# Loads of w, a, b for chunks 4 and 5 issued by ScalarE, and the first weight product placed behind chunk 0's state update

## The chip, the cores and the metric

The kernel runs on one core of a Trainium2 chip. A core has five instruction queues: PE (TensorE, matrix products), DVE (VectorE), ACT (ScalarE), POOL (GpSimd) and SP (SyncE, which here only issues transfers). Each queue works in order: an instruction that has to wait holds up everything behind it on that queue. Queues meet through semaphores. The metric is the device time of the kernel in microseconds (us), lower is better.

## The reference

Two blocks follow each other. The first is a recurrence with a 40 x 40 state per batch and head, over 768 steps, for 4 batches and 8 heads:

```
for t in range(S):
    y[:, :, t] = einsum('bhd,bhde->bhe', r_t, state)
    Sa = einsum('bhde,bhe->bhd', state, a_t)
    state = state * w_t[:, :, None, :] - outer(Sa, b_t) + outer(v_t, k_t)
```

The second takes y as 3072 tokens of 320 features and computes `h = x @ w_in`, `g = h * cos(h)`, `out = g @ w_out`, with 2048 hidden features. The six inputs of the recurrence are float32. The two weight matrices arrive as float64, so the kernel itself has to turn each pair of 32-bit words into a float32.

## The kernel before

**Tiling.** Time is cut into 24 chunks of 32 steps (`C = 32`, `NCH = 24`). A chunk's inputs lie in SBUF as 128 partitions (4 batches x 32 steps) by 8 heads x 40. Within a chunk the recurrence becomes matrix products, for which a 32 x 32 triangular system per batch and head must be inverted. That is done for four chunks at a time by 31 pairs of small DVE operations (`inv_step`, L464 to L472), which end in a transpose into the tile `rt` (L476).

**Stages of a chunk.** `p1_w`, `p1_a`, `p1_b`, `p1_n` prepare the decay, a, b and the triangular system, for two chunks at once. `p2_in` copies v and r to padded tiles on POOL (`vp`, `rp`, L490), `p2_kn` scales k and copies v on POOL (`kn`, `vvm`, L497 and L498), `p2_v`, `p2_k`, `p2_g` turn them and form the products inside the chunk (`gram`; ACT copies `vT`, `rT`, `kT`, L514 to L521; DVE `ag` L541; ACT and DVE `vvm`, L546 and L547). The chain from chunk to chunk is `ch_t` (turn the state `qz`: PE `sT`, ACT `s`, L562), `ch_q` (`qps`), `ch_x` (`x0ps`, copied by ACT L599 and DVE L600), `ch_s` (`sps`, with `rt`; copied to `sm` by ACT L617 and DVE L622), and `ch_z` (`dps`; DVE adds to the state, `qz` L656, POOL scales it, `qz` L657, and the outputs go to `yt`, L663 and L668).

**The second block** is cut into pieces (`first_a`, `first_b`, `second`), which an explicit list of segments puts between the stages of the recurrence. They are the bulk of PE's work: the groups `ph` and `po`.

**Weights.** Each of the two matrices is converted in pieces of 128 x 512 (`rounded`, L220). One piece takes a fetch of its words by SP (`fetch`, L233), `taken` (DVE L241 and L242, ACT L245 and L247), `mantissa` (DVE L251, ACT L254) and `product` (DVE L257, then POOL L260, which sets the sign). These steps form one list, `w_steps`, and `step(work, of_inv, of_w)` (L342) takes `of_w` of them after each segment. For chunks 0 and 1 that number is 4, the second entry of `fill = (1, 4)` (L924). So after `ch_s` of chunk 0 come taken 0, taken 1, mantissa 0 and product 0, and after its `ch_z` the next four.

**Order of the loads.** `later(n, work)` (L339) issues a piece of work after n further segments. `load(c, names, via)` (L146) issues four transfers of 40 KB for each named input of chunk c, by SP unless `via` says otherwise. k, v and r of all chunks share one tile each; `landed` (L501) asks for those of the next chunk once both readers on POOL are through. Two lines matter here:

```
elif c >= 2 and c + 3 < NCH:                       # L800
    for m in range(6):
        later(8 + m // 3 if c == 2 else ..., lambda m=m: load(c + 2 + m % 2, "wab"[m // 2]))
...
step(seg, *fill, small=seg in (q, x, g, s, z, pn, pn4))   # L982
```

With c == 2 the first loads w, a, b of chunks 4 and 5: w4, w5 and a4 after the eighth further segment, a5, b4 and b5 after the ninth. The decay w of these chunks comes from a table `wd` in DRAM, which SP stores shortly before (L180). Between the two groups SP fetches the words of the first three weight pieces, and k, v, r of chunk 2 stand behind all of it.

**Completion semaphores.** The program as built gives the transfers of SP and ACT eight completion semaphores in turn, and each transfer waits until the one that used its semaphore before has landed. So at most eight transfers of the two queues are under way, and either queue can wait for the other's.

`N_PAD` (L897) and `busy` (L856) put idle matmuls into PE's stream at the start: 111 tiny ones (`pad`) in front of the first `sps`, and some of 512 columns.

Of the kernel before, what the change touches and what calls it, by code (L numbers as in the profile page):

```python
# [20 lines left out]
def kernel(  # L21
# [43 lines left out]
    nc = tc.nc  # L65
# [54 lines left out]
    for n, fill in (("w", 1.0), ("a", 0.0), ("b", 0.0)):  # L120
        for i in range(4):
            x = slice((i - 2) * H * DP, (i - 1) * H * DP)
# [23 lines left out]
    def load(c, names, via=nc.sync):  # L146
        for n in names:
            for i in range(B):
                at_c = src[n][i, :, c * C : (c + 1) * C, :]
                if n == "w" and c >= 4:  # L150
                    at_c = wd[c // 4][i, :, c % 4]
                via.dma_start(nat[n, c][blk[i], :, :D], at_c.rearrange("h t d -> t h d"))  # L152
# [186 lines left out]
    def later(steps, work):  # L339
        waiting.append([steps, work])  # L340

    def step(work, of_inv=0, of_w=0, small=False):  # L342


        before = list(waiting)
        work()
        G["small"] = small
        for w in before:
            w[0] -= 1
            if w[0] == 0:  # L350
                waiting.remove(w)
                w[1]()
        for steps, n in ((inv_steps, of_inv), (w_steps, of_w)):
            for _ in range(min(n, len(steps))):
                steps.pop(0)()


    def p1_w(c):
        ps = at("wT")
        for i in range(2):  # L360
            turned(ps[:, i], nat["w", c + i])
        if c < 4:

            for i in range(2):
                nc.scalar.copy(G["w1"][:, i, :, 0:1], b4(ps[:, i])[:, :, 0:1])
            nc.vector.memset(ps[:, :, ::C], 0.0)
        for i in range(2):
            wb = ring.tile([P, 4 * P + 1], F32, tag="wb", name="wb")
            if c < 4:
                nc.vector.tensor_tensor_scan(  # L370
                    wb[:, 1:], ps[:, i], flat(G["w1"][:, i]), 0.0, ALU.mult, ALU.add
                )
            else:
                nc.scalar.copy(wb[:, 1:], ps[:, i])
            wc = ring.tile([P, 4 * B], F32, tag="wc", name="wc")
            nc.gpsimd.tensor_copy(wc, wb[:, C::C])
            G["wb", c + i], G["wx", c + i], G["wc", c + i] = wb, b4(wb[:, : 4 * P]), wc
            if c >= 4:
                from_one(c + i)
        if c == 8:  # L380
            later(2, lambda: over_w(c, unpad(nat["w", c])))
        elif c >= 4:
            over_w(c, unpad(nat["w", c]))
# [18 lines left out]
    def p1_a(c):  # L402
        if c >= 4:
            ps = at("aps")
            for i in range(2):
                turned(ps[:, i], nat["a", c + i])
            for i in range(2):
                a_W(c + i, ps[:, i])
            over_w(c + 1, unpad(nat["w", c + 1]))
            return  # L410
        for c in range(c, c + 2):
            wn = ps_h.tile([P, 512], F32, tag="h", name="wn")
            aps = ps_o.tile([P, 512], F32, tag="o", name="aps")
            for j in range(4):
                nc.tensor.transpose(
                    wn[:, j * P : (j + 1) * P], G["wb", c][:, j * P + 1 : (j + 1) * P + 1], ident
                )
            from_one(c)
            turned(aps, nat["a", c])
            over_w(c, unpad(wn.rearrange("p (h d) -> p h d", h=H)))  # L420
            a_W(c, aps)
# [364 lines left out]
    def p1(c):  # L786


        def first_w():
            p1_w(c)  # L790
            if c == 4:
                later(1, lambda: load(6, "w"))

        def both_a():
            p1_a(c)
            if c == 4:
                later(1, lambda: load(7, "w"))
                for i in range(2):
                    later(1, lambda i=i: load(6 + i, "ab"))
            elif c >= 2 and c + 3 < NCH:  # L800
                for m in range(6):
                    later(
                        8 + m // 3 if c == 2 else (9 if c == 6 else 2) + m, lambda m=m: load(c + 2 + m % 2, "wab"[m // 2])
                    )

        return [first_w, both_a, lambda: p1_b(c), lambda: p1_n(c)]
# [8 lines left out]
    def p2(c):  # L815
        def last():
            p2_g(c)
            if c + 1 < NCH:
                later(1, lambda: p2_in(c + 1))

        return [lambda: p2_v(c), lambda: p2_k(c), last]
# [9 lines left out]
    with tc.manual_schedule():  # L831
# [53 lines left out]
        v, k, g = p2(0)  # L885
# [34 lines left out]
        for c in range(NCH):  # L920
            t, q, x, s, z = main(c)
            v, k, g = p2(c + 1) if c + 1 < NCH else [lambda: None] * 3
            q0 = c - c % 4 + 4
            fill, pn, pn4 = (1, 4), None, None  # L924
            if c == 0:
                segs = [s, z]
            elif c == 1:
                segs = [t, v, q, k, x, g, s, z]
            elif c == 2:
                segs, fill = [t, v, q, k, M, x, M, g, M, s, M, z, M, M], (0, 2)  # L930
            elif c == 3:
                pw4, pa4, pb4, pn4 = p1(4)
                pw, pa, pb, pn = p1(6)
                segs = [
                    t, pw4, M, q, pa4, M, x, lambda: scanned(2), M, s, pw, M, pb4, pa, M, pn4, M, z, M,
                    pb, v, pn, k, M, g,
                ]
                fill = (2, 3)
            elif c == 4:
                pw, pa, *p8 = p1(8)  # L940
                segs = [t, v, M, q, M, k, x, M, M, M, M, pw, s, M, z, M, g, M, pa, lambda: scanned(3)]
                fill = (2, 0)
            elif c == 5:
                pw, pa = p1(10)[:2]
                pb, pn = p8
                segs = [t, M, pb, q, M, pn, k, M, x, M, s, pw, v, M, z, M, g, M, pa, M]
            elif c % 4 == 0 and q0 < NCH:
                pb, pn = p1(q0)[2:]
                segs = [t, v, M, q, M, k, x, M, g, M, s, pb, M, z, M, pn, M, M]
                if q0 + 4 < NCH:  # L950
                    segs.insert(-1, lambda: scanned(c // 4 + 2))
            elif c % 4 == 1 and q0 < NCH:
                pw, pa = p1(q0 + 2)[:2]
                segs = [t, M, pw, q, M, x, k, M, s, v, M, z, M, pa, M, g, M, M]
            elif c % 4 == 2 and q0 < NCH:
                pb, pn = p1(q0 + 2)[2:]
                segs = [t, M, pb, q, M, pn, v, M, x, M, s, k, M, g, M, z, M, M]
            elif c % 4 == 3 and q0 + 4 < NCH:
                pw, pa = p1(q0 + 4)[:2]
                segs = [t, M, pw, q, M, x, k, M, s, v, M, z, M, pa, M, g, M, M]  # L960
            else:
                segs = [t, v, M, q, M, x, k, M, g, M, s, M, M, z, M, M]
            n = len(segs)

            goal = 8 * (c + 1) - (18 if c < 19 else 20)
            empty, places = 0, segs.count(M)
            if c > 3:
                empty = max(0, min(places - (goal - done), 2 if c < 8 else places))
                goal = max(goal, done + places - empty)
            place = 0  # L970
            if c == 19:
                shifted(N_PAD[c])
            for i, seg in enumerate(segs):
                while seg is s and ("rt", c) not in G:
                    if allowed(c):
                        piece(4, 0)
                    else:
                        inv_steps.pop(0)()
                while seg is pn4 and w_steps:
                    w_steps.pop(0)()  # L980
                if seg is not M:
                    step(seg, *fill, small=seg in (q, x, g, s, z, pn, pn4))  # L982
                    if c < 2 or c == 2 and not done:
                        busy({s: 6, q: 5, v: 4, k: 4, z: 4}.get(seg, 3))
                else:
                    place += 1
                    if place * empty // places > (place - 1) * empty // places:
                        continue
                    if allowed(c) and (c != 4 or done < 23):
                        piece(*fill)  # L990
                while i == n - 1 and c > 3 and done < goal and c != 4 and allowed(c):
                    piece(*fill)
                if seg is pn and (c == 3 or c > 4 and c % 4 == 2):
                    inv_steps.extend(inverse(q0))
# [36 lines left out]
```

## Time and profile before

| | us |
|---|---|
| median of 3 runs | 825.33 (822.83 to 826.02) |
| span of the profiled execution | 823.7 |
| PE busy | 746.9 (91%) |
| DVE busy | 509.3 (62%) |
| ACT busy | 383.8 (47%) |
| POOL busy | 201.3 (24%) |

The profile's own execution took 823.7 us from its first to its last instruction, 1.6 below the median of the runs. A busy share is an average over stages with different limits: what a change in one stage is worth has to be read from that stage. The chain of waits follows the work that ended last back through what released it. The timeline lists instructions by start, with their length and the idle time of their engine ahead of them. "SPq" and "ACTq" are the transfers issued by those queues; issuing is not counted as busy. Numbers such as L152 are lines of the kernel.

### The profile page before, as it was taken

Reading aid. Unit: us, or ns where it says so; the run is one execution under the profiler, and the core shown is the slowest. Engines: PE = TensorE matmul, PEld = TensorE weight load, DVE = VectorE, ACT = ScalarE, POOL = GpSimd, SP = SyncE. Lnnn points to the kernel's source line nnn. Section 1 sums busy time; section 2 is a strip of 40 time slices with the busy share of each in tenths; the row PEclk is TensorE's granted clock in tenths of the full one; section 3 lists DMA queues with packets and bytes.
Section 4 is the critical chain, followed back from the end, with each engine's and each line's share of the span. In section 5 each row is a group of like instructions: output and inputs, shape, how many; then the busy total and the mean of one; then the engine's idle time right before and its main releaser. Section 6 shows DMA issues by size and latency. Waiting matters only on the chain.

```text
span 823.7 us, 37673 instructions
## 1 busy us (share of the span) xinstructions
PE 746.9 (91%) x16832; PEld 571.3 (69%) x16832; DVE 509.3 (62%) x1081; ACT 383.8 (47%) x707; POOL 201.3 (24%) x352
## 2 busy tenths in 40 slices
PE   3656778899689999999999999999999999999997
PEld 2534456677467777778777777777787777777775
DVE  6987887859645599354797553895444874332231
ACT  1214676544244553545446446435635445363352
POOL 5315554430214023212221230330330222201000
PEclk9757799899789999999999999999999999999999
DMA  8456663244043322333223323214310212101000
GB/s 120 78 132 168 173 162 104 46 119 69 25 98 84 64 59 52 69 100 65 54 37 71 68 63 67 61 37 65 66 41 24 45 35 52 21 21 37 20 17 16
DMA packets 183297, 55.66 MB, mean 68 GB/s; under 512 B 157152, under 2 KB 178656, under 8 KB 183136
## 3 DMA queue, kind: packets, MB, share of 16 engines
q1 hardware_dynamic: 180560, 51.95, 29.2%
q8 instruction: 132, 2.16, 1.1%
q10 hardware_dynamic: 2320, 0.98, 0.6%
q0 software_dynamic: 256, 0.33, 0.2%
q14 instruction: 29, 0.24, 0.1%
HBM read 42.07 MB, written 11.14 MB: 65 GB/s over the span
## 4 chain that ended last, share of the span: by engine, by line
PE 63%; DVE 19%; ACT 6%; DMA 4%; issue 3%; SPq 3%; POOL 1%; DVEq 0%; ACTq 0%; POOLq 0%
PE ph L101 22%; PE po L101 20%; DVE inv_tmp L468 4%; DVE inv L472 4%; PE x0ps L101 3%; PE dps L101 3%; SPq L152 3%; PE gram L101 2%; DVE rw L391 2%; PE vT L326 2%; PE sps L101 2%; PE qps L101 1%; DVE turns L732 1%; PE nps L101 1%; PE sT L558 1%
## 5 line engine op out<-in xcount | busy, mean ns | idle before, releaser
L101 PE MATMUL po<-w_out_sb,gT 128*128 128x320 f32 x768 | 227.0, 445 | 0.0
L101 PE MATMUL ph<-xT,w_in_sb 128*128 128x256 f32 x768 | 189.5, 393 | 4.8 <-DVE gT L740 3.8
L101 PEld LDWEIGHTS po<-w_out_sb,gT 128*128 128x128 f32 x768 | 142.4, 193 | 55.9 <-issue 4.2
L101 PEld LDWEIGHTS ph<-xT,w_in_sb 128*128 128x128 f32 x768 | 142.3, 194 | 33.9 <-issue 13.9
L730 ACT ACTIVATE turns<-ph,rnd 128x512 f32<-128x512 f32 x96 | 63.8, 685 | 157.2 <-PE ph L101 156.7
L732 DVE SCALAR_TENSOR_TENSOR turns<-turns,ph 128x512 f32<-128x512 f32 x96 | 63.8, 684 | 109.2 <-ACT turns L730 108.9
L740 DVE TENSOR_TENSOR gT<-ph,turns 128x512 f32<-128x512 f32 x96 | 65.6, 685 | 36.3 <-ACT turns L737 36.3
L657 POOL TENSOR_TENSOR qz<-qz,wc 128x160 f32<-128x160 f32 x92 | 43.2, 489 | 163.1 <-DVE qz L656 162.6
L472 DVE TENSOR_TENSOR inv<-inv,inv_tmp 128x31 f32<-128x31 f32 (+15 forms) x186 | 72.0, 387 | 6.4
L468 DVE TENSOR_TENSOR inv_tmp<-u,inv 128x31 f32<-128x31 f32 (+15 forms) x186 | 70.0, 376 | 4.4
L736 ACT ACTIVATE turns<-turns 128x512 f32<-128x512 f32 x96 | 60.2, 627 | 23.3 <-DVE turns L732 23.3
L737 ACT ACTIVATE turns<-turns,half_pi 128x512 f32<-128x512 f32 x96 | 69.3, 722 | 3.1
L490 POOL COPY vp<-nat_v 128x320 f32<-128x320 f32 x25 | 12.5, 501 | 182.9 <-DMA nat_v<-in_v_dram 144.1
L101 PE MATMUL ph<-xT,w_in_tail 64*128 64x256 f32 x384 | 54.8, 404 | 0.0
L656 DVE TENSOR_TENSOR qz<-dps,qz 128x160 f32<-128x160 f32 x92 | 28.9, 315 | 33.9 <-PE dps L101 33.8
L391 DVE RECIPROCAL rw<-nat_w 128x320 f32<-128x320 f32 x20 | 42.8, 2142 | 0.1
L562 ACT COPY s<-sT 128x512 f32<-128x512 f32 x46 | 24.5, 584 | 37.6 <-PE sT L558 37.6
L101 PEld LDWEIGHTS ph<-xT,w_in_tail 64*128 64x128 f32 x384 | 33.3, 187 | 10.4 <-issue 6.6
L668 POOL TENSOR_TENSOR yt<-yt,wb 128x512 f32<-128x512 f32 x24 | 31.3, 1306 | 22.4 <-DVE yt L663 22.4
L546 ACT COPY vvm<-gram 128x256 f32<-128x256 f32 x24 | 8.8, 368 | 55.6 <-DVE ag L541 55.3
L101 PEld LDWEIGHTS sps<-x,rt 32*32 32x32 f32 x1536 | 18.1, 109 | 21.6 <-issue 16.5
L101 PE MATMUL sps<-x,rt 32*32 32x72 f32 x1536 | 23.0, 240 | 10.7 <-DVE rt L476 9.0
(118 smaller groups left out, 1070.1 us busy)
## 6 DMA issues: line engine op xcount, KB each, us to landing
words<-in_moe_w_in_dram SPq DMA_DIRECT2D x8, 512.0 KB
nat_k<-in_k_dram SPq DMA_DIRECT2D x96, 40.0 KB
nat_v<-in_v_dram SPq DMA_DIRECT2D x96, 40.0 KB
nat_r<-in_r_dram SPq DMA_DIRECT2D x96, 40.0 KB
xd<-yt SPq DMA_DIRECT2D x48, 80.0 KB
out_dram<-ot SPq DMA_DIRECT2D x24, 160.0 KB
nat_b<-in_b_dram SPq DMA_DIRECT2D x88, 40.0 KB
wd<-ws SPq DMA_DIRECT2D x5, 640.0 KB
```

The costliest lines, as they stand in the source:

```text
L101: nc.tensor.matmul(o, lhsT=lhsT, rhs=rhs, start=start, stop=stop, skip_group_check=True)
L391: nc.vector.reciprocal(rw, wn)
L468: nc.vector.tensor_tensor(tmp, u[:, j : j + 1, :j].to_broadcast([P, C - j, j]), x[:, j:, j : j + 1].to_broadcast([P, C - j, j]), ALU.mult,)
L472: nc.vector.tensor_tensor(x[:, j:, :j], x[:, j:, :j], tmp, ALU.subtract)
L656: nc.vector.tensor_tensor(z, pick(dp, 0, (2 * N72 + C, 2), (N72, 2), (1, D)), z, ALU.add)
L657: nc.gpsimd.tensor_tensor(z, z, wc.rearrange("p (f m b) -> p f m b", f=2, m=2)[:, :, :, bb] .unsqueeze(3).to_broadcast([P, 2, 2, D]), ALU. ...
L668: nc.gpsimd.tensor_tensor(yt.rearrange("p j b t -> p (j b) t"), yt.rearrange("p j b t -> p (j b) t"), wx, ALU.mult)
L730: nc.scalar.activation(n, u, ACTF.Identity, bias=rnd, scale=1.0)
L732: nc.vector.scalar_tensor_tensor(n, n, -ROUND, u, ALU.add, ALU.subtract)
L736: nc.scalar.activation(n, n, ACTF.Abs)
L737: nc.scalar.activation(n, n, ACTF.Sin, bias=half_pi, scale=-2.0 * math.pi)
L740: nc.vector.tensor_tensor(gT[:, 2 * e : 2 * e + 2].rearrange("p f t -> p (f t)"), us[e], ns[e], ALU.mult)
```

## The change

Two edits. In `p1` the six loads for chunks 4 and 5 are issued by ACT instead of SP, and in pairs: w4, w5 after the eighth further segment, a4, a5 after the ninth, b4, b5 after the tenth. And after `ch_s` of chunk 0 one weight step less is taken, so that product 0 comes after `ch_z`, and every later weight step moves back by one place in the list of segments until the list is emptied.

```
--- before.py
+++ after.py
@@ -800,7 +800,8 @@
             elif c >= 2 and c + 3 < NCH:
                 for m in range(6):
                     later(
-                        8 + m // 3 if c == 2 else (9 if c == 6 else 2) + m, lambda m=m: load(c + 2 + m % 2, "wab"[m // 2])
+                        8 + m // 2 if c == 2 else (9 if c == 6 else 2) + m,
+                        lambda m=m: load(c + 2 + m % 2, "wab"[m // 2], nc.scalar if c == 2 else nc.sync),
                     )
@@ -979,7 +980,7 @@
                 while seg is pn4 and w_steps:
                     w_steps.pop(0)()
                 if seg is not M:
-                    step(seg, *fill, small=seg in (q, x, g, s, z, pn, pn4))
+                    step(seg, fill[0], fill[1] - (c == 0 and seg is s), small=seg in (q, x, g, s, z, pn, pn4))
```

In the program as built PE's stream is the same instruction for instruction. SP's loses 24 transfers, ACT's gains them: the eight of w stand behind chunk 0's copy of `x0ps` (L599), the eight of a behind chunk 1's `vT` and `rT`, the eight of b behind its `kT` and ahead of its `vvm` (L546). On SP the store of `wd` is now followed by the six fetches of the first three weight pieces and then by k, v, r of chunk 2. On DVE product 0 (L257) stands behind the four pairs L656 and L663 of chunk 0, on POOL its sign (L260) behind the four L657 and the L668. Further down one weight step of DVE or ACT changes places with the segment's own operation at each place where they meet.

## Prediction

> **What bounds the kernel now.** I read the page first, then the chain of waits, then the timelines of SP, ACT and DVE from 40 to 80 us. Two rows of the page, busy tenths in 40 slices of 20.6 us:
>
> ```profile
> PE   3656778899689999999999999999999999999997
> DVE  6987887859645599354797553895444874332231
> ```
>
> From the ninth slice on (165 us) PE is nearly full, a dip from 206 to 247 apart. A microsecond won before that moves PE's whole stream forward; later none is to be had from these edits. The chain of waits through the changed stage (start, us, what):
>
> ```profile
> 68.54 0.45 SPq L152
> 68.99 0.04 issue
> 69.03 2.51 DMA nat_r<-in_r_dram
> 71.61 0.08 issue
> 71.69 0.45 POOL rp L490
> 72.14 1.55 POOL w_in_sb L260
> 73.69 2.94 POOL qz L657 x4
> 76.64 0.04 issue
> 76.68 0.70 PE sT L558 x2
> ```
>
> POOL's scaling of the state stands behind a copy that waits for r of chunk 2, and behind the first weight's sign. Why r is late, on SP's timeline (start, length):
>
> ```profile
> 42.43 4.74 SPq L152 DMA_DIRECT2D nat_w<-wd  x8
> 47.26 1.87 SPq L152 DMA_DIRECT2D nat_a<-in_a_dram  x4
> 49.18 3.94 SPq L233 DMA_DIRECT2D words<-in_moe_w_in_dram  x6
> 53.22 3.69 SPq L152 DMA_DIRECT2D nat_a<-in_a_dram  x4
> 56.96 5.32 SPq L152 DMA_DIRECT2D nat_b<-in_b_dram  x8
> 62.37 1.88 SPq L152 DMA_DIRECT2D nat_k<-in_k_dram  x4
> ```
>
> SP issues without a pause, and 15.6 us of it (4.74 + 1.87 + 3.69 + 5.32) are the loads for chunks 4 and 5. Where they go, ACT's timeline:
>
> ```profile
> 47.75 0.59 ACT L515 COPY rT<-vT 128x512 f32<-128x512 f32 x1
> 51.10 0.58 ACT L521 COPY kT<-kT 128x512 f32<-128x512 f32 x1 [2.76 <-PE kT L326]
> 58.16 0.37 ACT L546 COPY vvm<-gram 128x256 f32<-128x256 f32 x1 [6.47 <-DVE ag L541]
> ```
>
> ACT is mostly idle between 45.7 and 58.2, but at 58.16 DVE waits for it inside its inversion:
>
> ```profile
> 58.56 0.42 DVE L547 TENSOR_TENSOR vvm<-gram,su 128x256 f32<-128x256 f32 x1 [0.44 <-ACT vvm L546]
> 61.18 1.91 DVE L476 STREAM_TRANSPOSE rt<-inv 128x1024 f32<-128x1024 f32 x1
> 69.44 0.69 DVE L257 TENSOR_TENSOR w_in_sb<-mant,expo 128x512 f32<-128x512 f32 x1 [1.95 <-ACT mant L254]
> 79.14 0.75 DVE L257 TENSOR_TENSOR w_in_tail<-mant,expo 128x512 f32<-128x512 f32 x1 [0.81 <-ACT mant L254]
> ```
>
> DVE is full up to 63.1, and 9.19 and 9.43 of 10 us busy in 70 to 80 and 80 to 90 (stage view). So two things run side by side: the state chain, which the chain of waits shows, and the weight work on DVE and ACT, which has little room and sets the order of ACT's copies for the state chain.
>
> [...] SP's time goes into issuing, at DMA shares of 0.40 to 0.57 from 45 to 51 us. [...] so a copy behind eight loads waits for all eight to be issued. The trace of before has this for ACT only at the start: its table load begins at 7.35 us, behind nine loads. [...] L241 takes 0.42 us alone and 1.37 at 72.61, while POOL runs.
>
> **SP's relief.** After `wd` (issued at 39.29) words 0 and 1 and half of piece 2 can go at once. The other half waits for words 0 and 1 by the completion semaphores. 1.25 MB behind the 640 KB of `wd`, which lands at 42.4, at 208 to 321 GB/s (51 to 57 us before): about 47. So k, v, r go out from about 48 to 55, and the last r lands near 57 (transfer of r in the chain: 2.5 us) instead of 71.5. POOL first needs to be free at 68.7. The wait goes, with some 11 us in reserve; this part costs nothing by itself.
>
> **Product 0 moved.** The last `dps` matmul ends at 68.35, yet DVE starts the state's addition at 70.05, after 1.95 us of waiting and 0.61 of product. Now it starts at 68.4, and POOL's scaling at 68.7 instead of 73.66: 4.9 earlier, 3.3 of it from the freed POOL, 1.6 from DVE. The state chain thus wins 4.9. DVE's weight work wins less. It loses the 1.95 and the 0.81 us of idling (the second comes from ACT, which waits 1.46 us for `sT`), and gets a new wait of 0.9 for `dps` (67.5 to 68.4): -1.9.
>
> **ACT's cost.** 24 issues now stand between 45.7 and `vvm`. Unhindered issues stand 0.49 us apart (nat_a at 47.71, 48.19, 48.69). Below that: ACT's first eight loads took 4.92 us, 0.615 each; SP's 30 from 42.43 to 62.23, stalls included, 0.66. The three copies `vT`, `rT`, `kT` take 0.48 each (47.27 to 47.75). `vvm` then starts at 45.7 + 24 x n + 1.4: 58.9, 61.9 and 62.9 for the three values, against 58.12 when DVE is ready for it. I take n = 0.58, thus 61.0, a delay d of 2.9: the two queues now share eight semaphores and the engines, so the ideal is out, but SP's share is only twelve loads and ends early. Behind `vvm` stands DVE: L547, the last four steps, `rt`, so `sps`, `sm`, `dps` and the first weight work all come 2.9 later. A second way gives the same: `kT` ends at 45.7 + 16 x 0.58 + 1.5 = 56.5 instead of 51.7, `gram` with it, and the pads behind it (53.31 to 58.88 before) and two pairs of idle matmuls end at 65.9 instead of 61.1; `sps` began at 63.24. That is 2.7, not additional. Bounds: d = 0.8 to 6, the upper with n = 0.71, where each load meets the other queue's landings.
>
> **The shift by one weight step.** Where the order changes: at 90.9 DVE waits for ACT's `x` before a product instead of after it, +0.6. At 107 `s` (L562), for which PE's `qps` waits 1.52, no longer stands behind an L254 (0.63) that itself starts 0.98 late, -1.6; PE's `x0ps` and `ph` up to 119.1 can follow, and at 118 the L730 and L732 pass an L254 and an L251, so that `gT` (L740), for which PE waits 3.76 at 124.1, keeps -1.4 of it. At 141 to 145 `s` and `wb`, which PE waits for (1.45 and 2.08), pass an L254: -0.65. From there DVE's order is the same within a step. Sum -1.5, and -3 to 0 if DVE and POOL meet otherwise than before.
>
> **The sum.** +2.9 - 1.9 - 1.5 = -0.5 us at about 147 us, from where PE runs on to 180 with one wait, and the inversion for chunk 4 starts behind it: the shift goes through to the end. The state chain itself comes only 4.9 - 2.9 = 2.0 earlier at `sT`, and little of that counts, because ACT's copies for it wait in the weight work's order (at 83.15 an L245 waits 1.17 for DVE, and `qz` at 84.33 stands behind it). Span 823.7 - 0.5 = 823.2; with the 1.6 by which the median stood above the profiled execution, **824.8**.
>
> **Rivals.** *The state chain decides* (0.22). If `sT` 4.9 us earlier frees ACT and DVE as well, and ACT issues at nearly 0.49, it is +0.8 - 4.9 - 1.5 = -5.6: 819.7. For it: the chain of waits does run through POOL here. Against: of 14 us DVE idles only 2.8. *ACT becomes the gate* (0.17), the one that ends slower: between `x` and `vvm` the loads go in step with SP's, each waiting for a landing. The result is slower by 0.5% (4.1 us) once d - 3.4 passes 4.1, that is when `vvm` starts after 65.6, n = 0.77 us a load. With n = 0.83 `vvm` starts at 67.0, d = 8.9, and 8.9 - 3.4 = +5.5: 830.8. For it: at the start, three queues together, POOL's loads took 3.2 to 6.3 us to land. Against: n = 0.615 for ACT at that same time. *Nothing to see* (0.06): k, v, r stay late because SP waits for the words, or gain and loss meet exactly: 825.3. The reserve of 11 us speaks against the first.
>
> **How the numbers follow.** The forecast has 0.55. Its own range takes d from 0.8 to 6, the shift from -3 to 0, and the runs' spread of 1.6 either way: 820.5 to 829. The rivals take it to 819 and 830.5. 0.5% is about what a measurement of this kernel can tell from no change. Faster by more: 0.05 of the forecast and 0.17 of the first rival, 0.22. Slower: 0.03 and 0.15, 0.18. Within: 0.60.
>
> **What would show it.** POOL's `vp` of chunk 2 before 60 instead of 69.6. ACT's `vvm` of chunk 1 at 61 (58.9 to 64), `rt` ending d later than 63.1, `sps` likewise. POOL's first L657 near 71.6. The weight product of the tail (L257, 79.14) within a microsecond of where it was. PE's `ph` at 124.1 and `aps` at 145.5 earlier by 0.5 to 2. Wrong if `vvm` comes past 65, if PE's pads end later than the inversion by more than a microsecond, or if the weight work turns out not to hold the state chain.

## The result, and the profile after

The changed kernel takes 832.02 us (median of 4 runs, 831.21 to 833.42) against 824.59 of the kernel before, measured beside it (822.83 to 826.02): a ratio of 1.0103 (95% interval 1.0077 to 1.0128), or +8.5 us (6.3 to 10.5). It is slower, and 832.0 lies above the range of 819 to 830.5. Its profiled execution took 830.9 us, 7.2 more than that of before. Differences given below in us are a kernel's ratio and its interval times 824.

Lines of the file behind the first edit are one higher than before; the lines named here lie ahead of it, except that the memset `tick` is L862 (L861 before).

The busy tenths of the changed kernel's page, in slices of 20.8 us:

```profile
PE   3537787789689999999999999999999999999997
...
DVE  6977886868754489454698454895444873332231
```

PE's digits are lower than before by one or two in the second and third slice (21 to 62 us) and by one in the seventh to ninth (125 to 187); the fourth and the sixth are higher by one. From the tenth on they agree with those of before, digit for digit. What is lost is lost before 187 us, and the kernel then ends 7.2 us later.

SP and POOL of the changed kernel, timelines (start, length, instruction, in brackets the idle time ahead of it):

```profile
39.49 8.49 SPq L233 DMA_DIRECT2D words<-in_moe_w_in_dram  x6
...
54.43 2.08 SPq L152 DMA_DIRECT2D nat_r<-in_r_dram  x4
```
```profile
55.96 0.46 POOL L490 COPY vp<-nat_v 128x320 f32<-128x320 f32 x1 [12.08 <-DMA nat_v<-in_v_dram]
58.91 0.46 POOL L490 COPY rp<-nat_r 128x320 f32<-128x320 f32 x1 [2.50 <-DMA nat_r<-in_r_dram]
73.59 1.74 POOL L657 TENSOR_TENSOR qz<-qz,wc 128x160 f32<-128x160 f32 x4 [14.22 <-DVE qz L656]
```

k, v and r of chunk 2 are issued by 56.5 instead of 69.5, and POOL's `vp` runs at 55.96 instead of 69.60. POOL then idles 14.22 us until DVE has the first part of the new state: its first L657 starts at 73.59, where it was 73.66 before. The four L657 end 1.3 earlier (75.33), and PE's `sT` behind them 1.5 earlier (75.83 instead of 77.37). ACT's copy `s` of it loses this again. It stands behind a conversion (L245) that waits 1.64 us for DVE, while ACT idles and `sT` is there, and comes 3.7 later than before (81.14 instead of 77.41); PE's `qps`, which did not wait before, waits 4.03 us for it. The state chain has won nothing. ACT in the kernel before, then ACT and PE in the changed one, timelines:

```profile
77.41 1.07 ACT L562 COPY s<-sT 128x512 f32<-128x512 f32 x2 [1.46 <-PE sT L558]
```
```profile
79.95 0.72 ACT L245 ACTIVATE expo<-expo,to_bits 128x512 int32<-128x512 int32 x1 [1.64 <-DVE expo L242]
...
81.14 1.05 ACT L562 COPY s<-sT 128x512 f32<-128x512 f32 x2
```
```profile
82.24 1.29 PE L101 MATMUL qps<-rT,s 40*40 40x32 f32 x64 [4.03 <-ACT s L562]
```

The chain of waits of the changed kernel through the same stage now runs over ACT's transfers (start, us, what):

```profile
57.41 0.04 ACT kT L521
57.49 0.33 ACTq L152
...
62.51 0.04 issue
62.55 0.38 ACT vvm L546
62.95 0.42 DVE vvm L547
...
65.60 1.92 DVE rt L476
...
67.65 1.25 PE sps L101 x64
```

And ACT and DVE, timelines:

```profile
45.91 5.26 ACTq L152 DMA_DIRECT2D nat_w<-wd  x8
...
51.75 0.59 ACT L515 COPY rT<-vT 128x512 f32<-128x512 f32 x1
...
57.41 0.59 ACT L521 COPY kT<-kT 128x512 f32<-128x512 f32 x1 [5.08 <-DMA nat_a<-in_a_dram]
57.49 5.01 ACTq L152 DMA_DIRECT2D nat_b<-in_b_dram  x8
62.55 0.37 ACT L546 COPY vvm<-gram 128x256 f32<-128x256 f32 x1 [4.55 <-DMA nat_b<-in_b_dram]
```
```profile
62.95 0.42 DVE L547 TENSOR_TENSOR vvm<-gram,su 128x256 f32<-128x256 f32 x1 [2.89 <-ACT vvm L546]
...
65.60 1.91 DVE L476 STREAM_TRANSPOSE rt<-inv 128x1024 f32<-128x1024 f32 x1
...
73.18 0.33 DVE L656 TENSOR_TENSOR qz<-dps,qz 128x160 f32<-128x160 f32 x1 [1.27 <-PE dps L101]
...
82.86 0.68 DVE L257 TENSOR_TENSOR w_in_tail<-mant,expo 128x512 f32<-128x512 f32 x1
```

`kT` ends 6.3 us later than before, `vvm` starts at 62.55 instead of 58.16, `rt` at 65.60 instead of 61.18, and the weight product of the tail (L257) at 82.86 instead of 79.14. So 4.4 us are missing at 65 us and 3.7 at 83; at 91 us (DVE's `x`, L600) it is 2.7, and then it grows again: the second `gT` (L740), at 124.5 before, comes 6.5 later. A second loss lies between 91 and 125 us, where none was forecast.

### The profile page after: what moved, and what is told of

It is laid out like the page before. It is cut to its first block, busy times and chain, and to the rows that moved or that the text cites. A ratio compares the mean times of both kernels' runs of the same rounds, so it can differ in the third digit from the quotient of the medians.

```text
span 830.9 us, 37673 instructions
## 1 busy us (share of the span) xinstructions
PE 745.6 (90%) x16832; PEld 569.3 (69%) x16832; DVE 513.3 (62%) x1081; ACT 384.5 (46%) x707; POOL 201.0 (24%) x352
## 3 DMA queue, kind: packets, MB, share of 16 engines
q10 hardware_dynamic: 8848, 1.97, 1.3%
q8 instruction: 132, 2.16, 1.1%
## 4 chain that ended last, share of the span: by engine, by line
PE 63%; DVE 19%; DMA 5%; ACT 5%; issue 4%; SPq 2%; POOL 1%; ACTq 1%; DVEq 0%; POOLq 0%
PE ph L101 22%; PE po L101 19%; DVE inv_tmp L468 4%; DVE inv L472 4%; PE dps L101 3%; PE x0ps L101 3%; DVE rw L391 3%; PE gram L101 2%; PE vT L326 2%; PE sps L101 2%; PE nps L101 2%; PE qps L101 1%; SPq L152 1%; DMA ws<-in_w_dram 1%; DVE turns L732 1%
## 5 line engine op out<-in xcount | busy, mean ns | idle before, releaser
L730 ACT ACTIVATE turns<-ph,rnd 128x512 f32<-128x512 f32 x96 | 64.1, 686 | 159.5 <-PE ph L101 159.2
L740 DVE TENSOR_TENSOR gT<-ph,turns 128x512 f32<-128x512 f32 x96 | 65.7, 686 | 36.3 <-ACT turns L737 36.3
L657 POOL TENSOR_TENSOR qz<-qz,wc 128x160 f32<-128x160 f32 x92 | 42.1, 476 | 181.3 <-DVE qz L656 180.7
L656 DVE TENSOR_TENSOR qz<-dps,qz 128x160 f32<-128x160 f32 x92 | 29.2, 317 | 34.5 <-PE dps L101 34.4
L562 ACT COPY s<-sT 128x512 f32<-128x512 f32 x46 | 24.5, 583 | 36.1 <-PE sT L558 36.1
L101 PEld LDWEIGHTS ph<-xT,w_in_tail 64*128 64x128 f32 x384 | 33.4, 188 | 10.1 <-issue 6.5
L668 POOL TENSOR_TENSOR yt<-yt,wb 128x512 f32<-128x512 f32 x24 | 31.7, 1319 | 22.6 <-DVE yt L663 22.6
L546 ACT COPY vvm<-gram 128x256 f32<-128x256 f32 x24 | 8.8, 368 | 55.2 <-DVE ag L541 50.3
```

Source lines behind the costliest of these rows:

```text
L101: nc.tensor.matmul(o, lhsT=lhsT, rhs=rhs, start=start, stop=stop, skip_group_check=True)
L656: nc.vector.tensor_tensor(z, pick(dp, 0, (2 * N72 + C, 2), (N72, 2), (1, D)), z, ALU.add)
L657: nc.gpsimd.tensor_tensor(z, z, wc.rearrange("p (f m b) -> p f m b", f=2, m=2)[:, :, :, bb] .unsqueeze(3).to_broadcast([P, 2, 2, D]), ALU. ...
L668: nc.gpsimd.tensor_tensor(yt.rearrange("p j b t -> p (j b) t"), yt.rearrange("p j b t -> p (j b) t"), wx, ALU.mult)
L730: nc.scalar.activation(n, u, ACTF.Identity, bias=rnd, scale=1.0)
L740: nc.vector.tensor_tensor(gT[:, 2 * e : 2 * e + 2].rearrange("p f t -> p (f t)"), us[e], ns[e], ALU.mult)
```

## The experiments

Two theories to begin with. *Gate*: the 24 issues delay ACT's `vvm`, and all of the loss grows from that. *Two parts*: the delay costs about half, and the other half comes from the weight steps standing one place further back ("the lag" below).

**One edit at a time.** `loads_only` has the first edit alone, `prod_only` the second alone:

```
loads_only:  step(seg, *fill, small=...)                              # as before
prod_only:   8 + m // 3 if c == 2 else ..., load(..., "wab"[m // 2])  # as before, by SP
```

> Only the first edit: the loads for chunks 4 and 5 on ACT, weight steps placed as before. Two theories share out the 7 us that the whole change lost. Gate: the 24 issues on ACT delay vvm of chunk 1 by some 4 us, and all of the loss grows from that delay; then this kernel loses 6 to 8 us, about as much as the change itself. Two parts: the delay gives about 4 (rt ending near 66 to 67.5, and the tail product L257 at 82 to 83 instead of 79.1), the rest comes from the place of the weight steps; then this kernel loses 3 to 4.5. Both expect ACT's vvm copy at 62 to 63 instead of 58.2.

> Only the second edit: one weight step less after chunk 0's s, loads on SP as before. r of chunk 2 then still lands near 71.6, and vvm stays near 58.2. Two parts: one step later for every weight step costs 2.5 to 4 us by itself, seen as DVE waiting for ACT's x (L600) and PE's ph near 118 coming late. Gate: the place of the steps costs nothing or gains, -2 to +0.5. My forecast's terms gave -1.5 for the shift.

Measured: `loads_only` 827.22 against 823.99, ratio 1.0043 (1.0031 to 1.0056), +3.5 us; `prod_only` 828.68, ratio 1.0054 (1.0033 to 1.0075), +4.5 us. The two add up to 8.0, the change itself cost 8.5. The gate theory falls: the weight steps cost by themselves, with `vvm` in time. In `loads_only` `vvm` came at 60.94 and `rt` ended at 65.89, both a little ahead of what was expected of it.

**The loads on SP, behind k, v, r.** `sp_late` gives SP's relief without ACT's issues, `sp_late_prod` adds the second edit:

```
-    8 + m // 3 if c == 2 else ...
+    12 + m if c == 2 else ...          # still by nc.sync
```

> The loads stay on SP, but each pair of four goes one segment later, the first after the twelfth further segment, so that k, v, r of chunk 2 and the words are issued first; weight steps as before. SP's relief without ACT's issues. Expected: POOL's vp of chunk 2 before 60, vvm at 58.2, POOL's first L657 at 70 to 71.5 instead of 73.7. If the state chain (POOL waiting for r) holds anything, the time falls by 2 to 3.5 us; if the weight work on DVE and ACT holds it, the time stays within 1 us.

> As the one before it (loads on SP behind k, v, r), and one weight step less after chunk 0's s: the whole change without ACT's issues. Gate: with the delay of vvm gone, -2 to -4 us (my forecast's -1.9 and -1.5). Two parts: +2 to +4, the cost of the place of the weight steps alone. In both POOL's first L657 should come near 68.7 to 69.5, as the state's addition no longer stands behind product 0.

Measured: `sp_late` 824.53, ratio 1.0000 (0.9987 to 1.0012); `sp_late_prod` 829.05, ratio 1.0055 (1.0035 to 1.0074), +4.5 us. In `sp_late` POOL's `vp` runs at 51.73 and its first L657 at 70.92, 2.7 us earlier than before, and the time does not move: the state chain, which the chain of waits showed, is not what holds this stage. In `sp_late_prod` the first L657 comes at 70.03, later than expected. And the lag costs the same 4.5 us with the loads early or late on SP. `sp_late` is the base of most kernels below.

**Product 0 or the lag?** The second edit does two things: product 0 goes behind chunk 0's state update, and every later step stands one place further back. `sp_late_nolag` takes the step back after `ch_z`, `lag_from_x1` keeps product 0 where it was and starts the lag at 90 us, and `lead` goes one place the other way:

```
sp_late_nolag:  fill[1] - (c == 0 and seg is s) + (c == 0 and seg is z)
lag_from_x1:    fill[1] - (c == 1 and seg is x)
lead:           fill[1] + (c == 0 and seg is s)
```

> Loads on SP behind k, v, r; one weight step less after chunk 0's s and one more after its z. Product 0 stands behind the state update, and every later step is where it was before. If the 4.5 us that the second edit costs come from the later steps standing one place further back, they are gone: within 1.5 us of before. If they come from product 0 behind the state update, they stay: +3.5 to +5.

> Loads on SP behind k, v, r; product 0 ahead of the state update as before; the one step less is taken after chunk 1's x, so that only the steps from there on (90 us) stand one place further back. Later steps decide: +2.5 to +4.5, with L241 and L242 of the step after chunk 1's state update near 104 to 109 late, and ACT's copies of vT, rT (L514, L515) and PE's kT and ph behind them. Product 0 decides: within 1 us of before.

> Loads on SP behind k, v, r; one weight step more after chunk 0's s, so that every later step stands one place further forward than before. If what counts is only that a ready step covers DVE's waits for ACT and PE, one place forward covers at least as many: -2 to 0. If the places are matched to ACT, whose copies for the recurrence then stand behind one more conversion, it costs like the step backward: +1 to +4.

Measured: `sp_late_nolag` 824.27, ratio 0.9999 (0.9982 to 1.0015); `lag_from_x1` 826.70, 1.0030 (1.0017 to 1.0043), +2.5 us; `lead` 829.25, 1.0065 (1.0042 to 1.0087), +5.4 us. Product 0 behind the state update costs nothing and brings nothing. All of the 4.5 us is the lag, and one place forward costs as much or more: the places are matched to their surroundings on both sides. In `lead` PE waits 2.77 us for ACT's `s` (L562) before chunk 2's `qps`, 1.52 before.

Why product 0 brings nothing is on DVE's timeline of `sp_late_nolag`:

```profile
68.16 0.33 DVE L656 TENSOR_TENSOR qz<-dps,qz 128x160 f32<-128x160 f32 x1 [1.90 <-PE dps L101]
...
69.88 0.97 DVE L257 TENSOR_TENSOR w_in_sb<-mant,expo 128x512 f32<-128x512 f32 x1
```

The wait for ACT's mantissa that stood ahead of product 0 (1.95 us) has become a wait of 1.90 for `dps`; the product, 0.69 long before, takes 0.97 beside POOL's L657.

**Where the lag costs.** Three kernels put the start or the end of the lag elsewhere, one swaps the product and the mantissa ahead of chunk 1's state update without any lag:

```
lag_to_x1:    fill[1] - (c == 0 and seg is s) + (c == 1 and seg is x)
lag_from_s1:  fill[1] - (c == 1 and seg is s)
lag_from_z1:  fill[1] - (c == 1 and seg is z)
swap_s1:      if c == 1 and seg is s:
                  w_steps[1:4] = [w_steps[3], *w_steps[1:3]]
```

> Loads on SP behind k, v, r; one weight step less after chunk 0's s, one more after chunk 1's x: only the steps between chunk 0's state update and chunk 1's x (66 to 91 us) stand one place further back. If the two halves of the lag cost separately (4.6 in all, 2.5 of it from chunk 1's x on), +1.5 to +2.5. If the first half is made up again before PE needs it, within 0.8 us of before, and then the cost of the whole lag is more than the sum of its halves.

> Loads on SP behind k, v, r; the one weight step less is taken after chunk 1's s, so that only the step next to its state update, and those behind it, stand one place further back. If what costs from x of chunk 1 on is that the mantissa step (L251) falls behind the state update, so that L241, L242, ACT's vT and rT and PE's kT come late: +1.5 to +3, like the lag from chunk 1's x. If it is the product that no longer covers the wait before L600: within 0.8 us of before.

> Loads on SP behind k, v, r; the step less is taken only after chunk 1's z, so that the steps in front of chunk 1's state update are those of before. If the place next to that update is what costs (the lag from chunk 1's s lost 2.3), 0 to +0.8. If the later places cost, +1.5 to +2.5.

> Loads on SP behind k, v, r, no lag; of the four weight steps between chunk 1's s and z, the mantissa step (L251) goes ahead of the product (L257), so that the product and its sign on POOL (L260) stand right in front of the state update, as the lag puts them. If POOL's L657 behind L260 is what the lag costs there, it starts near 102 and not 100.5, with L668, kn and the transposed tokens behind it: +1 to +2.3. If it is L251 standing behind the update instead of in front of it (which is not so here), within 0.6 us of before.

Measured: `lag_to_x1` 1.0007 (0.9991 to 1.0023), +0.6; `lag_from_s1` 1.0027 (1.0010 to 1.0045), +2.2; `lag_from_z1` 1.0010 (0.9989 to 1.0031), +0.8; `swap_s1` 0.9997 (0.9983 to 1.0011), -0.2. The medians fit that about half of the cost comes in with the one mantissa step that changes sides at chunk 1's state update (2.2 with it, 0.8 from the next place on), but the two intervals overlap, so this is not shown. It is not POOL: with product and sign right in front of the update (`swap_s1`) POOL's first L657 starts at 101.65 instead of 100.52 in `sp_late`, and nothing is lost. Nor is it what I had expected of `lag_from_s1`: its time fits, its reason doesn't. There L242, for which ACT's conversion waits, starts at 105.60, against 106.19 in `sp_late`; by then that trace is 0.7 early (chunk 1's `sm`, L622), so it is 0.1 late and no more.

No single place holds the whole. Set beside `sp_late`, `sp_late_prod` is 0.5 us late at `rt`, before the edit acts, 1.0 at chunk 1's `x` (L600, 90 us), 1.6 at its `sm` (99 us), 3.2 at chunk 2's `x` (119 us), 3.5 at the first `gT` (125 us) and 4.6 at chunk 3's `x` (159 us) and at the end. This is one profiled execution of each.

What happens between 99 and 119 us, the largest of these steps, is seen on PE. The kernel before, timeline from chunk 2's `qps` on:

```profile
108.41 0.84 PE L101 MATMUL qps<-rT,s 40*40 40x32 f32 x64 [1.52 <-ACT s L562]
...
111.33 0.63 PE L326 MATMUL kT<-ident,kn 128*128 128x128 f32 x4 [0.90 <-issue]
...
112.66 1.89 PE L101 MATMUL ph<-xT,w_in_sb 128*128 128x256 f32 x8
114.48 0.88 PE L101 MATMUL x0ps<-vvm,ag 32*32 32x72 f32 x64
...
124.14 3.65 PE L101 MATMUL ph<-xT,w_in_sb 128*128 128x256 f32 x8 [3.76 <-DVE gT L740]
```

The same work in `prod_only`:

```profile
108.30 0.82 PE L101 MATMUL qps<-rT,s 40*40 40x32 f32 x64
...
112.80 0.63 PE L326 MATMUL kT<-ident,kn 128*128 128x128 f32 x4 [2.49 <-issue]
...
114.37 3.44 PE L101 MATMUL ph<-xT,w_in_sb 128*128 128x256 f32 x8
117.74 0.88 PE L101 MATMUL x0ps<-vvm,ag 32*32 32x72 f32 x64
...
127.90 3.50 PE L101 MATMUL ph<-xT,w_in_sb 128*128 128x256 f32 x8 [4.26 <-DVE gT L740]
```

In the kernel before PE waits twice: 1.52 us for `s`, then 0.90 for `kT`. In `prod_only` `s` no longer stands behind an L254, so that `qps` doesn't wait for it; it runs at 108.30 although PE's `sT` (L558) ends 1.5 later, at 105.99. But `kT` comes 1.5 later. It follows ACT's copy `rT` (L515), which ends 0.1 us ahead of it before and in the five kernels with the long wait, and which stands behind the conversion L245 and L247, which waits for DVE. That has not become faster: with a mantissa step now behind the state update, DVE's L242 starts at 109.28 instead of 107.80. Two waits have become one of 2.49, nearly the same length in five kernels with the lag at chunk 1's update (`prod_only`, `sp_late_prod`, `lag_from_x1`, `lag_from_s1` and, with 2.50, the change itself). And then the eight `ph` take 3.44 instead of 1.89. The granted clock says why. Stretches of 2 us of `prod_only` (length and PE's busy us, in brackets its instructions, then clock, DMA share, GB/s):

```profile
112.00:114.00 2.00, 1.20 (x8) 0.99 0.30 68
114.00:116.00 2.00, 2.00 (x6) 0.50 0.60 118
116.00:118.00 2.00, 2.00 (x37) 0.66 0.87 235
```

and of the kernel before:

```profile
112.00:114.00 2.00, 2.00 (x11) 1.00 0.45 74
114.00:116.00 2.00, 2.00 (x131) 1.00 0.86 254
```

The clock falls to half after the long wait. The `ph` ahead of `x0ps` took 1.89 to 1.97 us in the fourteen kernels where `kT` and `ph` wait less than 1 us, and 2.30, 3.21, 3.44 and 2.48 in `lag_from_s1`, `lag_from_x1`, `prod_only` and the change; `sp_late_prod` kept 1.97, and there PE waited 0.35 for the transposed tokens instead. At `gT` PE waits 3.5 to 3.8 us in the kernels with the old places there and 4.25 or 4.26 with the lag: ACT's second L730 then waits 1.24 us for this late `ph` (in `sp_late_prod` and the change), where it stood behind an L254 before.

The clock's record in the traces shows where the falls begin and end. In `prod_only` half clock lasts, among others, from 93.47 to 96.89, from 100.30 to 103.71, from 113.95 to 117.37 and from 127.61 to 131.02: all of these times are whole steps of 3.41 us apart. In every other trace they are too, but the steps lie elsewhere: in the changed kernel's the stretches of half clock between 50 and 160 us last 20.48, 6.83, 10.24, 3.41, 6.83 and 3.41 us, and one of them begins at 115.89. A whole step of idling was not needed. Of the steps at full clock in the twenty traces, from 30 to 800 us, 3820 had less than 1 us without a PE instruction, and none of them was followed by half clock. Of 148 with 1 to 2 us, 42 were, and of 115 with over 2 us, 113. In the traces of before and of the change alone it is none of 380, 4 of 11 and 13 of 13. In the kernel before, a pause of 1.73 ahead of `dps` (97.66 to 99.38) was followed by half clock from 100.34 on.

The wait for `kT` was followed by half clock in four of five profiled executions. In those four, 2.25 to 2.50 us of it lay within one step. In `sp_late_prod` it lasted from 109.67 to 112.17, and a step ended at 110.45. In the changed kernel the wait (113.20 to 115.70) lies in a step at full clock that ends at 115.89; the next step, to 119.30, has 0.50, the one behind it 1.00. The fall explains `ph` in `prod_only`, 3.44 us instead of 1.89, but not the lag's cost: `sp_late_prod` kept full clock at this place, lost the same 4.5 us by its median, and its profiled execution was 4.6 longer than that of `sp_late` (825.6 against 821.0). The profiled execution of `prod_only` was the slowest of its six runs (832.06).

**Moving the wait.** If PE's wait for `kT` were the way by which the lag costs, the copies `vT` and `rT` ahead of ACT's conversion would take it off. Two steps of chunk 2 go from behind `t` to behind `v`, once without and once with the lag:

```
t2_zero:      fill[1] + 2 * (c == 2) * ((seg is v) - (seg is t))
lag_t2_zero:  the same, and - (c == 0 and seg is s)
```

> Loads on SP behind k, v, r, no lag; the two weight steps after chunk 2's turn of the state (t) are taken after its v instead, so that ACT copies vT and rT before it converts. PE's kT (109.7) then waits only for POOL's kn: about 107.1. If PE's wait for kT is on the way to ph, x0ps and gT, these come 1 to 2.5 us earlier and the time falls by 0.5 to 2.5; if the weight products hold gT anyway: 0 to +1.

> The same two steps moved behind v of chunk 2 in the kernel with the whole lag (loads on SP), which lost 4.5. If the lag's cost at 108 to 123 runs through ACT's conversion ahead of vT and rT to PE's kT (112.2 there), kT comes near 109.6 and 2 to 3 us of the 4.5 are won back: +1.5 to +2.5. If it runs through the weight products to gT, the loss stays: +4 to +5.

Measured: `t2_zero` 0.9995 (0.9980 to 1.0010), -0.4; `lag_t2_zero` 1.0041 (1.0024 to 1.0059), +3.4. `t2_zero` does what it should at `kT`, which follows without a wait, and `ph` starts 0.9 us earlier than in `sp_late`; but `gT` comes at 121.55 instead of 121.69, and PE waits 4.47 for it: without the lag the weight work on DVE and ACT holds `gT`. With the lag, another wait stands in the same place:

```profile
108.89 0.66 PE L326 MATMUL kT<-ident,kn 128*128 128x128 f32 x4
...
112.47 3.19 PE L101 MATMUL ph<-xT,w_in_sb 128*128 128x256 f32 x8 [2.07 <-DMA xT<-xd]
```

`ph` waits for the transposed tokens instead, and again takes long, 3.19 us where it took 1.89 in the kernel before; the wait of 2.07 lay within one step. The difference to the 4.5 of `sp_late_prod` lies within the intervals: inconclusive on how much was won back. It does show that behind `kT` another wait is nearly as late. That neither kernel gains at the end what it gains at `kT` leaves the way of the lag's cost open.

**How ACT's loads cost.** `act_w_a` leaves only the sixteen loads of w and a on ACT, so that `vvm` is in time; two more kernels take pads out of PE's way:

```
act_w_a:        (8 + m // 2 if m < 4 else 12 + m) if c == 2 else ...
                nc.scalar if c == 2 and m < 4 else nc.sync
act_w_a_pads:   N_PAD = {0: 40, 19: 75}          # 111 before
act_w_a_pads2:  shifted(40) at the old place, shifted(N_PAD[0] - 40)
                behind the loop over inv_steps
```

> Only the sixteen loads of w and a on ACT, those of b on SP behind k, v, r; weight steps as before. Which way the ACT loads cost: if through ACT's vvm (DVE waits for it), nothing is left, because vvm can start at 45 + 16 x 0.63 + 1.4 = 56.5 and DVE asks at 58.1: within 1 us of before. If through kT, gram and the pads behind them on PE (kT ends near 56.3 as in the kernel with all 24 on ACT), sps comes 1.5 to 3 us later and the kernel loses 1.5 to 3.

> As the kernel with w and a on ACT and b on SP, with 40 tiny pads instead of 111 in PE's stream before chunk 0's sps (1.9 us less there; they compute nothing). If the sixteen loads cost their 2.6 us through kT, gram and the pads, behind which a DVE memset (L862) waited for PE inside the inversion, most of it goes: within 1 us of before, rt ending near 63 and not 65.4. If they cost it elsewhere, it stays at +2 to +3.

> w and a on ACT, b on SP; 40 pads at the old place and the other 71 behind the inversion's idle matmuls, so that PE has as many instructions as before. If the 17 us that the kernel with 40 pads lost came from the shorter stream, they are gone. If the sixteen loads cost through the pads, the 2.6 us shrink to 0 to 1; if through kT and gram alone, they stay at 2 to 3.

Measured: `act_w_a` 826.50, 1.0032 (1.0017 to 1.0047), +2.6. `vvm` starts at 58.78, 0.6 later than before, and `rt` at 63.45, 2.3 later. PE and DVE of `act_w_a`, timelines:

```profile
56.73 0.84 PE L101 MATMUL gram<-aT,kT 40*32 40x32 f32 x60 [6.11 <-ACT kT L521]
...
60.47 1.49 PE L101 MATMUL pad<-idle 128*1 128x1 bf16 x54 [0.69 <-issue]
61.82 0.58 PE L863 MATMUL busy<-idle,tick 128*1 128x512 bf16 x1
```
```profile
59.18 0.42 DVE L547 TENSOR_TENSOR vvm<-gram,su 128x256 f32<-128x256 f32 x1 [0.44 <-ACT vvm L546]
...
62.45 0.22 DVE L468 TENSOR_TENSOR inv_tmp<-u,inv 128x60 f32<-128x60 f32 x1 [1.79 <-issue]
...
63.45 1.91 DVE L476 STREAM_TRANSPOSE rt<-inv 128x1024 f32<-128x1024 f32 x1
```

`kT` is late, so `gram` and the pads are, and inside the inversion DVE waits 1.79 us at the second memset of `tick`, until the first idle matmul behind the pads has read it. That is the forecast's "second way".

`act_w_a_pads` gave 841.48, 1.0215 (1.0189 to 1.0241), +17.7 us: an experiment that changed something else. In the stage itself it did what was meant: no wait at the memset, and from `kT` to `rt` 5.7 us instead of 7.4. The 17 us arise far behind it: 1.5 of them are there at 155 us, 4.8 at 480 and 15.6 at 757, while PE pauses at places where none of the edits is (ten pauses over 0.5 us behind 250 us, 10.1 us in all, against four and 2.4 in `act_w_a`). With the 71 pads put back elsewhere (`act_w_a_pads2`) it is 826.27, 1.0014 (0.9992 to 1.0035), +1.2: the 17 us go with the shorter stream of PE.

The traces show where these pauses stand. Behind 170 us `act_w_a_pads` has nine pauses of 0.69 to 1.82 us that neither `act_w_a` nor the kernel before has, 9.8 us together. Ahead of every one of them stands a number of PE instructions, its semaphore waits counted, that leaves 193 or 194 when divided by 256. A reading of this, as an estimate: the pages of the kernel before, of the change and of `act_w_a_pads` have 132 packets of kind "instruction" (q8), 2.16 MB in all, in the traces 16,384 bytes each. Spread over the 33,664 matmuls and weight loads on the page of before that is about 64 bytes each, so some 256 instructions a packet. The pauses would then stand at edges between packets, and 142 instructions fewer (71 pads with their weight loads) move other work to every later edge. That PE waits there for a packet, and why at these places and not at others, was not tested.

The interval of `act_w_a_pads2` holds both 0 and 2.6, so this pair settles the pads' share only by the trace.

**Both costs in the change, and the free edits together.**

```
no_lag:    the change, and + (c == 0 and seg is z)
best_try:  sp_late_nolag, and the two steps of t2_zero
```

> The changed kernel with one weight step more after chunk 0's z: loads on ACT, product 0 behind the state update, every later step at its old place. If the two costs add up, the lag's 4.6 us go and the loads' 3.5 stay: +2.5 to +4.5. If the two stand in each other's way, the time is outside that.

> Loads on SP behind k, v, r; product 0 behind the state update; later steps at their old places, but the two behind chunk 2's t moved behind its v. Each of the three edits measured within 0.6 us of before; together, if their small gains at PE's kT and at the state chain meet: -0.5 to -2; if the weight work holds the way to gT: -0.5 to +0.5.

Measured: `no_lag` 827.56, 1.0056 (1.0036 to 1.0077), +4.6; `best_try` 823.14, 1.0000 (0.9982 to 1.0018). With the lag taken away the change keeps the cost of its loads, a little over the upper end of what was expected, with an interval that includes the 3.5; 3.9 of its 8.5 us go. That the two costs add up fits, within these intervals. Nothing found beats the kernel before.

## Why the prediction was wrong

It was +2.9 for ACT, -1.9 for product 0, -1.5 for the shift, together -0.5. The runs give +3.5 (`loads_only`), -0.1 (`sp_late_nolag`) and +4.5 (`prod_only`, `sp_late_prod`; 3.9 between the change and `no_lag`), together 7.9, against 8.5 for the whole. Of the signs that the forecast named, `vp` (55.96) and `vvm` (62.55) came as it said; the first L657 (73.59, not 71.6), the tail's product (3.7 later, not within 1) and `ph` (6.5 later, not 0.5 to 2 earlier) did not.

- *SP's relief*: right. r is there before it is wanted, and alone it is worth nothing (`sp_late` 1.0000).
- *ACT's cost*: right in mechanism, and in size within its bounds of 0.8 to 6. In `loads_only` `vvm` starts at 60.94, forecast 61.0. In the change it is 62.55, because eight loads took 5.26 and 5.01 us, 0.66 and 0.63 each instead of 0.58, and 0.5 of the 4.4 was there already at `x` (L599, 45.84). The second way, over `kT` and the pads, is real: with the first taken away it still cost 2.6 (`act_w_a`). The second alone was not taken away.
- *Product 0 moved*, -1.9: mis-sized, it is -0.1. The term took a wait of 0.9 for `dps` in exchange for 1.95 and 0.81. Measured, it was 1.27 in the change, 1.90 in `sp_late_nolag` and 2.05 in `sp_late_prod`, and the product itself took 0.97 beside POOL. The idle time was moved, not removed.
- *The shift by one weight step*, -1.5: this is the step that failed, in sign. It looked at the places where an ACT copy passes a conversion, and the first of these came true: `s` comes earlier and `qps` waits no longer. But "PE's `x0ps` and `ph` up to 119.1 can follow" was wrong. `kT` stands between, and it waits for `rT`, which stands behind a conversion that had not become earlier: the 1.52 saved at `qps` came back as a wait of 2.5 at `kT`, where it had been 0.90. The step also priced what the weight work loses at one place only, where it no longer covers a wait of DVE. At chunk 1's `x` that was right: L600 waits 1.69 instead of 1.13 for ACT, forecast +0.6. At chunk 2's `x` it waits 2.35 instead of 0.76, and nothing had been put there.
- *The state chain comes earlier at `sT`*, 2.0 by the sum: `sT` began 0.1 and ended 1.5 earlier. That little of it counts was right, and for the reason given: ACT's copy of it stood behind a conversion that waits for DVE, and came 3.7 later. `sp_late`, whose L657 came 2.7 earlier, was no faster.
- *The rivals.* "ACT becomes the gate" had the right sign. Its place was right and its price wrong: by its own threshold, `vvm` after 65.6, it should not have decided at 62.55. It explains 3.5 of the 8.5. "The state chain decides" falls. No case held a cost for the lag: it was given a range of -3 to 0, and so the whole range missed. Its own bounds for d and the shift with the spread of 1.6 reach from 819.6 to 831.0, more than the 820.5 to 829 that it took from them; the result lies outside these too.

Still open: how the lag's 4.5 us divide, and by which waits they reach the end. Its halves measured +0.6 and +2.5, 3.1 in all, and the missing 1.4 lie within the sum of the intervals. The wait for `kT` and the fall of PE's clock are read from traces; `sp_late_prod` has the cost without the fall.

## What to carry to other kernels

Moving one step in an order shared by several engines moves all that follow, so test it by giving the step back one segment later: here that one term separated an edit that costs nothing from a lag that costs 4.5 us. When an operation is forecast to come earlier, find the next one on the same engine and what that waits for: a gain in front of a wait that stays only makes the wait longer (PE's for `kT`, 2.49 us instead of 0.90). And a transfer issued by a computing engine is paid by whatever stands behind it there: in `loads_only` 24 issues of 0.58 to 0.60 us cost 3.5 us, although ACT had idled for 10.8 us at that place before.

## What was not expected of the hardware

PE's clock fell to half after pauses well under a step of 3.41 us: behind the 1.73 us ahead of `dps` in the kernel before it was 0.50 from 100.34 to 103.75. What went with the falls in the twenty traces is how much of a step PE idled (half clock behind none of 3820 steps with less than 1 us, behind 113 of 115 with over 2), and where the steps lie differs from one execution to the next: the same wait of 2.49 us had half clock behind it in `prod_only` and not in `sp_late_prod`. So one profile can show a cost of some 1.5 us (`ph`, 3.44 instead of 1.89) at a place where the next one need not have it.

And 71 tiny matmuls fewer in PE's stream made the kernel 15 us slower than the same kernel with them (`act_w_a_pads` against `act_w_a`), by pauses of 0.69 to 1.82 us, 193 or 194 PE instructions past a multiple of 256 and hundreds of us behind the place. The kernel before has such pauses too: the 1.24 us inside `gram` (88.38 to 89.62) and the 1.14 inside `sps` (92.76 to 93.89), which its timeline puts down to "issue", have 2497 and 2753 PE instructions ahead of them, and both numbers leave 193. Comparing kernels whose PE streams differ in length by even that much is not safe here.
